# A long convolution and routed experts on one core: result copies of the first group's 48-point stage on ScalarE, sums of the third group's first 20 items on VectorE, and a filter image of 96 rows

## The chip, the cores and the metric

The kernel runs on one core of a Trainium2 chip. A core has five engines that work side by side, each with its own queue of instructions that it takes in order: TensorE (PE; its weight loads are listed as PEld), VectorE (DVE), ScalarE (ACT), GpSimd (POOL) and SyncE (SP), which here issues most of the transfers between the chip's main memory and the on-chip memory (SBUF). 16 DMA engines carry all transfers. TensorE writes to PSUM, a small memory of banks; VectorE and ScalarE read it, GpSimd's work here reads SBUF. The metric is the device time of one execution in microseconds (us); the figure is the median of the runs.

## The reference

```python
def _attn_ref(x, h):                     # x: 8 x 5696 x 128, h: 5696 x 128
    L = 2 * S
    Xf = np.fft.rfft(x, n=L, axis=1)
    Hf = np.fft.rfft(h, n=L, axis=0)
    Yf = Xf * Hf[None, :, :]
    return np.fft.irfft(Yf, n=L, axis=1)[:, :S, :]

def _moe_ref(x, w_gate, w1, w2):         # x: 45568 x 128, 8 experts, 1024 hidden
    logits = x @ w_gate
    expert_idx = np.argmax(logits, axis=1)
    ...                                  # gate_w: softmax weight of the chosen expert
    for e in range(E):
        mask = expert_idx == e
        xe = x[mask]
        h = np.maximum(xe @ w1[e], 0.0)
        out[mask] = gate_w[mask, None] * (h @ w2[e])
```

A causal convolution of each of 8 sequences with a filter of the same length, and then, for each of the 45,568 rows, one of 8 two-layer experts.

## The kernel before, in words

The transform of length 11,424 is cut into two factors, 48 points and 238 points, of which 120 frequencies q are kept. The 8 sequences are three groups of 2, 3 and 3 (256, 384 and 384 columns, 128 for each sequence). For each group come three stages. Stage A (`phase_a`) multiplies by the long factor and stores the result to U in main memory. Stage B (`phase_b`), the 48-point stage, has 120 items, one for each q: it takes U, transforms over 48 points, multiplies by the filter's transform, transforms back and stores to V. Stage C (`phase_c`) takes V, undoes the long factor, computes which expert each row belongs to and scatters the rows in order of expert to a table SR. The experts (`moe`) then take tiles of 256 rows from SR.

One item of stage B goes through these steps, each some items behind the first (`BLAGS`):

- `forward` (L467): TensorE multiplies the item's slice of uq by its 96 x 128 matrix mt into a PSUM bank, xp. The 128 rows are two halves of 64 (real and imaginary part), of which 48 carry data and 16 are zero.
- `product` (L492, L495): VectorE multiplies xp by the filter image hh, once whole into zt (128 rows) and twice by halves, crossed, into xs (64 rows each).
- `combine` (L502): zt = zt + xs, on GpSimd.
- `inverse` (L510): TensorE multiplies zt by mi into a bank, vp.
- `save` (L519): vp is copied to vt in SBUF, on VectorE in the first group and on ScalarE in the others. After every fourth item vt goes to V (L555).

xp and vp share four banks in turn, so a forward multiply waits for the products two items back and an inverse multiply for the copy two items back.

The first group's stage B also makes the filter image. For a block of four items `filt` (L438) multiplies the filter's transform uht by mt, and `filt_save` (L448) copies each block's result in four pieces on ScalarE to one of three buffers hh. The buffer is used at once by the products and stored to HS in main memory (L555). Groups two and three load it from there, one transfer for each block of four items (L425):

```python
HS = dram.tile([P, QN, 2, D], F32, name="HS")
...
nc.sync.dma_start(hhs[qb][:, :QB], HS[:, q : q + QB])
```

The three buffers are set to zero at the start, all 128 rows. The transfers of a block, 512 KB for hh beside 384 or 576 KB for uq and V, 192 KB for mt and twice 72 KB for mi, all go through SyncE's one queue, in the order in which they are written; it waits there for whatever a transfer needs.

The order of all queues is written by generators that are run against one another by nominal costs (`run`). Beside the first group's stage B runs `weights`, which splits the expert weights into two parts (a cast on ScalarE, L230, a subtraction on VectorE, L231) and stores them to WD. The third group's stage B starts after the second group's last scatters have been put on GpSimd's queue (`sort_one`, L581); from some 20 items on, its items alternate with the second group's expert tiles (xr are their rows, loaded at L935, wb their weights from WD, L954; L985 is the first layer).

Of the kernel before, what the change touches and what calls it, by code (L numbers as in the profile page):

```python
# [13 lines left out]
F32 = mybir.dt.float32  # L14
# [4 lines left out]
ALU = mybir.AluOpType  # L19
# [4 lines left out]
NB = 48  # L24
MB = 119
QN = 120
MP = 120
HP = 64
# [14 lines left out]
SAVEV = ()  # L43
# [5 lines left out]
GAPS = (0, 6000, 5000)  # L49
HOLD = (0, 0, 0)  # L50
AHEAD = 2
HEAD = 26000
A3 = (True, True, False)
ALO = ('gpsimd', 'vector', 'vector')
# [11 lines left out]
def conv_moe(ctx: ExitStack, tc: tile.TileContext, I, out, B, S, D, E, F, split):  # L66
    nc = tc.nc
    P = 128
    K2 = 2 * NB
# [6 lines left out]
    def pool(name, bufs, space=None):  # L76
        kw = {} if space is None else {"space": space}
        return ctx.enter_context(tc.tile_pool(name=name, bufs=bufs, **kw))

    dram = pool("dram", 1, DRAM)  # L80
# [54 lines left out]
    for g, nbs in enumerate(split):  # L135
# [7 lines left out]
            parts.append(gr.parts[-1])  # L143
            b0 += nb
        groups.append(gr)
    HS = dram.tile([P, QN, 2, D], F32, name="HS")
    WD = dram.tile([4, E * P, F], F32, name="WD")

    queue = []
# [248 lines left out]
    def phase_b(gr):  # L398
        g, cb, cw, nch, QB = gr.g, gr.cb, gr.cw, gr.nch, gr.qb
        tiles, outs_ = {}, {}  # L400
# [13 lines left out]
        def load(qb):  # L414
            q = qb * QB
            if q >= QN:
                return
            uq = sb.tile([K2, QB, gr.cols], F32, tag="ld", name=f"uq{g}_{q}", bufs=LD if g else 3)
            nc.sync.dma_start(uq, gr.U[q : q + QB].rearrange("q p c -> p q c"))
            mi = mibufs[qb % 4]  # L420
            for k in range(2):
                nc.sync.dma_start(mi[k * HP : k * HP + NB], I["miq"][k * NB : (k + 1) * NB, q : q + QB, :])
            if g != 0:
                hhs[qb] = hhbufs[qb % 3]
                nc.sync.dma_start(hhs[qb][:, :QB], HS[:, q : q + QB])  # L425
            tiles[qb] = (uq, mi)

        mats, hhs, hbank, cuts = {}, {}, {}, {}
        cutting = F3[g]
        state, banks, late = {}, {}, []  # L430
# [9 lines left out]
        def filt_save(qb, m):  # L440
            if qb not in hbank:
                return
            hp = hbank[qb]
            if m == 0:
                hhs[qb] = hhbufs[qb % 3]
            hh = hhs[qb]
            c2, k = divmod(m, 2)
            nc.scalar.mul(hh[k * HP : (k + 1) * HP, :, c2, :], hp[c2 * HP : (c2 + 1) * HP], -1.0 if m == 3 else 1.0)  # L448
            if m == 3:
                hbank.pop(qb)  # L450
                late.append((HS[:, qb * QB : qb * QB + QB], hh[:, :QB]))

        def forward(n):
            q, c = items[n]
# [44 lines left out]

        def combine(n):  # L500
            zt, xs = state[n]
            nc.gpsimd.tensor_tensor(out=zt, in0=zt, in1=xs, op=ALU.add)  # L502

        def inverse(n):
            q, c = items[n]
# [7 lines left out]
        def save(n):  # L513
            q, c = items[n]
            qb, k0 = divmod(q, QB)
            if k0 == 0 and c == 0:
                outs_[qb] = sb.tile([K2, QB, gr.cols], F32, tag="six", name=f"vt{g}_{q}", bufs=SIX)
            cp = nc.vector.tensor_copy if g == 0 or n % 4 in SAVEV else nc.scalar.copy
            cp(outs_[qb][:, k0, c * cw : (c + 1) * cw], banks.pop(n)[:K2, :cw])  # L519
            if k0 == QB - 1 and c == nch - 1:  # L520
                late.append((gr.V[qb * QB : qb * QB + QB].rearrange("q p c -> p q c"), outs_.pop(qb)))
                tiles.pop(qb), hhs.pop(qb), mats.pop(qb)
# [4 lines left out]
        for qb in range(3 if g == 0 else 2):  # L527
            load_m(qb)
            if qb < 2:
                load(qb)  # L530
# [4 lines left out]
        for m in range(4):  # L535
            filt_save(0, m)
# [4 lines left out]
        for n in range(N + BLAGS[3] + 2):  # L541
            qb, k0 = divmod(n, per)
            if k0 == 1:
                load_m(qb + (3 if g == 0 else 2))
            if k0 == min(3, per - 1):
                load(qb + 2)
            if k0 == 0:
                filt(qb + 1, QB - 1)
                if qb:
                    filt_save(qb, 3)  # L550
            else:
                filt(qb + 2, k0 - 1)
                filt_save(qb + 1, k0 - 1)
            while late:
                nc.sync.dma_start(*late.pop(0))  # L555
            if n < N:
                forward(n)
            cut(n + CUT)
            dp, dc, di, ds_ = BLAGS
            if 0 <= n - di < N:  # L560
                inverse(n - di)
            if 0 <= n - dp < N:
                product(n - dp)
            if 0 <= n - dc < N:
                combine(n - dc)
            if 0 <= n - ds_ < N:
                save(n - ds_)
            yield max(cw * 7 / 2.4 + 200, 2 * cw / 0.96 + 300) if g == 0 else RATE[3 * g - 2] * cw * 8 / 2.4
# [29 lines left out]
    def phase_c(pt, guest=None):  # L598
# [27 lines left out]
        def divide(n, k):  # L626
            if not pt.c3 or n >= nu:
                return
            src = vqs[n][:, :, k * cw : (k + 1) * cw]
            vr = sb.tile([QN, 2, 2, cw], F32R, tag="six", name=f"vr{g}_{n}_{k}", bufs=SIX)  # L630
            nc.scalar.copy(vr[:, 0], src)  # L631
            nc.vector.tensor_tensor(out=vr[:, 1], in0=src, in1=vr[:, 0].bitcast(F32), op=ALU.subtract)  # L632
            vrs[n, k] = vr
# [15 lines left out]
        def settle(n, k):  # L649
            if k == 0:  # L650
                rt = sb.tile([MP, NI, nb, RW], F32, tag="rt", name=f"rt{g}_{n}", bufs=6)
                nc.vector.tensor_tensor(
                    out=rt[:, :, :, D + 1].bitcast(I32),
                    in0=idb[:, pt.b0 : pt.b0 + nb].rearrange("p (o b) -> p o b", o=1).broadcast_to([MP, NI, nb]),
                    in1=ioff[:, n * NI : (n + 1) * NI].rearrange("p (i o) -> p i o", o=1).broadcast_to([MP, NI, nb]),
                    op=ALU.add,
                )
                rts[n] = rt.rearrange("p i b w -> p (i b) w")
            done = nc.scalar.copy(
                rts[n][:, k * cb : (k + 1) * cb, :D],  # L660
                ybank.pop((n, k))[:MP, :cw].rearrange("p (b d) -> p b d", d=D),
            )
            sort_one(done.ins)
# [127 lines left out]
        if gr.g:  # L791
            yield GAPS[2]
        for k in range(AHEAD):
            divide(*divmod(k, nsub))
# [4 lines left out]
        for n in range(n_end + 1):  # L799
            for k in range(nsub):  # L800
# [18 lines left out]
                if n < nu:  # L819
                    divide(*divmod(at + AHEAD, nsub))  # L820
                    settle(n, k)
# [287 lines left out]
    def rest():  # L1109
        yield from phase_a(groups[1])  # L1110
        wait = []
        for gr in groups[1:]:
            spent = 0
            for cost in phase_b(gr):
                spent += cost
                yield cost
                if spent > HEAD and wait:
                    wait.pop().ready = True
# [137 lines left out]
```

## Time and profile before

| | |
|---|---|
| median of 3 runs | 2405.68 us (2403.33 to 2406.07) |
| the profiled execution | 2400.84 us |
| its span, first to last instruction | 2399.1 us |
| mean granted TensorE clock | 0.951 |
| TensorE, VectorE, ScalarE, GpSimd busy | 89%, 67%, 44%, 47% |
| first group's stage B | about 114 to 344 us |
| second group's stage B | about 545 to 832 us |
| third group's stage B | about 1134 to 1470 us |
| the experts alone | from about 1770 us |

A row of a timeline has a start and a length in us, the engine ("SPq" is SyncE's queue), the line, the operation, what it writes and reads, the shapes and a count; in brackets stands how long the engine sat idle before it and what ended that. A row of a group has the count, then the group's busy time in us, the mean length of one in ns and the engine's idle time before them. A row on one line of the code has minimum, median and maximum in ns. A row of the windows has the stretch, each engine's busy time in it, the granted clock, the share of time in which the 16 DMA engines were busy and the rate that they moved.

### The profile page before, as it was taken

How to read it: one execution, taken by the hardware profiler on the slowest of the kernel's cores; microseconds unless marked ns; L12 is line 12 of the kernel's file. 1: busy time of each engine (PE TensorE's matmuls, PEld its weight loads, DVE VectorE, ACT ScalarE, POOL GpSimd, SP SyncE). 2: the span in 40 equal slices, each digit the busy share in tenths (PEclk: the TensorE clock that was granted, in tenths of full speed). 3: DMA queues.
4: the chain of work that ended last, by engine and by line, in shares of the span. 5: the costliest groups of instructions: out<-in, count | busy, mean ns of one | idle time of the engine just before them, and what ended most of it. 6: DMA issues, size and time to landing. Idle time of an engine off the chain costs nothing.

```text
span 2399.1 us, 46517 instructions
## 1 busy us (share of the span) xinstructions
PE 2125.5 (89%) x13998; PEld 1759.0 (73%) x13998; DVE 1602.7 (67%) x3987; ACT 1049.3 (44%) x2233; POOL 1136.7 (47%) x1161
## 2 busy tenths in 40 slices
PE   7777759767999989998699998999979999999997
PEld 4654435444777777775377777988878999999997
DVE  3599965456999846667688885676654455555554
ACT  4533315432443445553144444665534444444443
POOL 5333323663555516677545553577762233333332
PEclk8899989878999999998799999999989999999998
DMA  9988879779999768877778775566322222222220
GB/s 268 294 256 266 271 205 321 234 214 265 271 269 276 213 191 248 258 234 218 220 202 252 210 236 148 124 167 175 95 87 85 76 74 81 75 79 75 80 75 30
DMA packets 226940, 444.88 MB, mean 185 GB/s; under 512 B 30993, under 2 KB 141639, under 8 KB 226688
## 3 DMA queue, kind: packets, MB, share of 16 engines
q1 hardware_dynamic: 202752, 394.78, 56.4%
q0 software_dynamic: 23936, 47.09, 6.5%
q8 instruction: 115, 1.88, 0.3%
q14 instruction: 137, 1.12, 0.2%
HBM read 597.98 MB, written 175.89 MB: 323 GB/s over the span
## 4 chain that ended last, share of the span: by engine, by line
PE 61%; DMA 12%; issue 6%; DVE 4%; POOL 2%; SPq 2%; ACT 1%; POOLq 0%; DVEq 0%; ACTq 0%
PE mh L985 18%; PE ma L1005 18%; PE vp L510 5%; PE xp L467 5%; DMA wb<-WD 5%; PE yp L644 5%; PE pa L279 3%; PE mx L167 2%; DMA SR<-rt,pi 2%; DMA xt<-x 2%; PE tp L683 1%; PE tp L167 1%; POOL out L1028 1%; DVE xs L495 1%; POOL SR L581 1%
## 5 line engine op out<-in xcount | busy, mean ns | idle before, releaser
L993 DVE SCALAR_TENSOR_TENSOR hs<-mh,hs 128x512 fp32r<-128x512 f32 x728 | 502.6, 691 | 473.4 <-ACT hs L991 467.6
L985 PE MATMUL mh<-xtb,wb 128*128 128x256 f32 x4368 | 728.8, 303 | 41.4 <-DMA wb<-WD 30.4
L985 PEld LDWEIGHTS mh<-xtb,wb 128*128 128x128 f32 x4368 | 596.6, 192 | 127.6 <-issue 66.2
L1028 POOL DMA_INDIRECT out<-xr x364 | 362.7, 996 | 681.1 <-DVE xr L1019 606.2
L1005 PE MATMUL ma<-hs,wb 128*128 128x256 f32 x4368 | 659.9, 287 | 10.4 <-DMA wb<-WD 10.2
L991 ACT ACTIVATE hs<-mh 128x512 fp32r<-128x512 f32 x728 | 435.3, 598 | 520.4 <-PE mh L985 518.3
L1005 PEld LDWEIGHTS ma<-hs,wb 128*128 128x128 f32 x4368 | 577.4, 192 | 14.4 <-DMA wb<-WD 13.9
L581 POOL DMA_INDIRECT SR<-rt,pi x384 | 397.3, 1035 | 208.5 <-issue 68.5
L502 POOL TENSOR_TENSOR zt<-zt,xs 128x384 f32<-128x384 f32 (+1 forms) x360 | 324.9, 916 | 313.2 <-DVE xs L495 303.5
L495 DVE TENSOR_TENSOR xs<-xp,hh 64x384 f32<-64x384 f32 (+1 forms) x720 | 367.8, 511 | 26.3 <-POOL zt L502 14.8
L467 PE MATMUL xp<-uq,mt 96*128 96x384 f32 (+1 forms) x720 | 284.1, 478 | 84.4 <-DVE xs L495 53.0
L510 PE MATMUL vp<-zt,mi 128*96 128x384 f32 (+1 forms) x720 | 269.9, 456 | 19.4 <-POOL zt L502 17.2
L519 ACT COPY vt<-vp 96x384 f32<-96x384 f32 x240 | 114.1, 475 | 358.3 <-PE vp L510 349.2
L467 PEld LDWEIGHTS xp<-uq,mt 96*128 96x128 f32 x720 | 118.8, 197 | 133.3 <-PE hp L438 60.9
L492 DVE TENSOR_TENSOR zt<-xp,hh 128x384 f32<-128x384 f32 (+1 forms) x360 | 183.3, 509 | 39.8 <-PE xp L467 19.5
L510 PEld LDWEIGHTS vp<-zt,mi 128*96 128x96 f32 x720 | 108.8, 164 | 113.4 <-issue 58.0
L279 PE MATMUL pa<-xc,fcr 120*120 120x512 f32 x360 | 110.6, 446 | 32.1 <-ACT xc L257 12.4
L448 ACT ACTIVATE hh<-hp 64x512 f32<-64x512 f32 x120 | 70.9, 591 | 142.4 <-issue 100.9
L644 PE MATMUL yp<-vr,gcr 120*120 120x384 f32 x576 | 117.0, 338 | 0.0
L632 DVE TENSOR_TENSOR vr<-vq,vr 120x768 fp32r<-120x768 f32 x96 | 91.5, 955 | 34.2 <-ACT vr L631 33.7
L279 PEld LDWEIGHTS pa<-xc,fcr 120*120 120x120 f32 x360 | 68.0, 203 | 59.0 <-ACT xc L257 17.2
L644 PEld LDWEIGHTS yp<-vr,gcr 120*120 120x120 f32 x576 | 96.2, 183 | 0.3 <-DVE vr L632 0.3
(121 smaller groups left out, 2028.3 us busy)
## 6 DMA issues: line engine op xcount, KB each, us to landing
wb<-WD SPq DMA_DIRECT2D x728, 512.0 KB
vq<-V SPq DMA_DIRECT2D x64, 720.0 KB
U<-ut SPq DMA_DIRECT2D x48, 720.0 KB
uq<-U SPq DMA_DIRECT2D x60, 576.0 KB
V<-vt SPq DMA_DIRECT2D x60, 576.0 KB
hh<-HS SPq DMA_DIRECT2D x60, 512.0 KB
xr<-SR SPq DMA_DIRECT2D x182, 130.0 KB
xt<-x SPq DMA_DIRECT2D x96, 240.0 KB
```

The source lines that it names most:

```text
L279: nc.tensor.matmul(banks[m][:QN, :], lhs, rhs, start=(k == 0), stop=(k == len(ops) - 1))
L467: nc.tensor.matmul(xp[:, :cw], mt[:, k0, :], uc, start=True, stop=True)
L495: nc.vector.tensor_tensor(out=xs[to], in0=x3[at], in1=hv[at, 1].broadcast_to([HP, cb, D]), op=ALU.mult)
L502: nc.gpsimd.tensor_tensor(out=zt, in0=zt, in1=xs, op=ALU.add)
L510: nc.tensor.matmul(vp[:K2, :cw], mi[:, k0, :], zt.rearrange("p b d -> p (b d)"), start=True, stop=True)
L581: s = nc.gpsimd.indirect_dma_start(out=SR[:, :], out_offset=IndirectOffsetOnAxis(ap=pi[:, b : b + 1], axis=0), in_=rt[:, b, :], in_offset= ...
L644: nc.tensor.matmul(yp[:MP, :cw], lhs, rhs, start=(m == 0), stop=(m == len(ops) - 1))
L985: nc.tensor.matmul(hp[:, u, :], wb[:, a, f, :], xt[:, b, :], start=(n == 0), stop=(n == 2))
L991: done = nc.scalar.activation(hs[:, 0], hp, AF.Relu)
L993: nc.vector.scalar_tensor_tensor(out=hs[:, 1], in0=hp, scalar=0.0, in1=hs[:, 0].bitcast(F32), op0=ALU.max, op1=ALU.subtract)
L1005: nc.tensor.matmul(accs[j], wb[:, a, f, :], hs[:, b, u, :], start=(k == 0 and u == 0 and n == 0), stop=(k == NPAIR - 1 and u == 1 and n == 2),
L1028: sc = nc.gpsimd.indirect_dma_start(out=out[:, :], out_offset=IndirectOffsetOnAxis(ap=xr[:, s, D + 1 : D + 2].bitcast(I32), axis=0), in_=x ...
```

## The change

Three things. In the first group's stage B the copy of the result, vp to vt, moves from VectorE to ScalarE, as in the other groups. In the third group's stage B the sum zt + xs of items 0 to 19 moves from GpSimd to VectorE. And the filter image in main memory keeps the 2 x 48 rows that carry data, without the 2 x 16 zero rows: it is stored and loaded in two transfers of 48 rows (192 KB each) in place of one of 128.

```diff
+ALONE = 20
...
-    HS = dram.tile([P, QN, 2, D], F32, name="HS")
+    HS = dram.tile([2, NB, QN, 2, D], F32, name="HS")
...
-                nc.sync.dma_start(hhs[qb][:, :QB], HS[:, q : q + QB])
+                for k in range(2):
+                    nc.sync.dma_start(hhs[qb][k * HP : k * HP + NB, :QB], HS[k, :, q : q + QB])
...
-                late.append((HS[:, qb * QB : qb * QB + QB], hh[:, :QB]))
+                for k2 in range(2):
+                    late.append((HS[k2, :, qb * QB : qb * QB + QB], hh[k2 * HP : k2 * HP + NB, :QB]))
...
-            nc.gpsimd.tensor_tensor(out=zt, in0=zt, in1=xs, op=ALU.add)
+            eng = nc.vector if g > 1 and n < ALONE else nc.gpsimd
+            eng.tensor_tensor(out=zt, in0=zt, in1=xs, op=ALU.add)
...
-            cp = nc.vector.tensor_copy if g == 0 or n % 4 in SAVEV else nc.scalar.copy
-            cp(outs_[qb][:, k0, c * cw : (c + 1) * cw], banks.pop(n)[:K2, :cw])
+            nc.scalar.copy(outs_[qb][:, k0, c * cw : (c + 1) * cw], banks.pop(n)[:K2, :cw])
```

How it moves instructions is seen at three places. In the rows, the number behind a tile's name is the item (zt_13_0 belongs to item 13, vt_8 to the block that starts at item 8), or for hp the block; hh_106 to hh_108 are the three buffers. Lines of the changed kernel stand up to three higher.

VectorE in the first group's stage B, items 12 to 14, before:

```order
L492 TENSOR_TENSOR zt_12_0_1263<-xp_12_0_1241,hh_106 128x256
L495 TENSOR_TENSOR xs_12_0_1262<-xp_12_0_1241,hh_106 64x256 x2
L519 COPY vt_8_1268<-vp_8_0_1243 96x256
L492 TENSOR_TENSOR zt_13_0_1277<-xp_13_0_1258,hh_106 128x256
L495 TENSOR_TENSOR xs_13_0_1276<-xp_13_0_1258,hh_106 64x256 x2
L519 COPY vt_8_1268<-vp_9_0_1260 96x256
```

ScalarE at the same place, before:

```order
L448 ACTIVATE hh_107<-hp_4_1189 64x4x128 x4
L448 ACTIVATE hh_108<-hp_5_1254 64x4x128 x4
L230 CAST wsp_0_1379<-wraw_1036 128x512
L448 ACTIVATE hh_106<-hp_6_1319 64x4x128 x4
L448 ACTIVATE hh_107<-hp_7_1384 64x4x128 x4
```

and ScalarE now:

```order
L450 ACTIVATE hh_107<-hp_4_1192 64x4x128
L522 COPY vt_8_1272<-vp_8_0_1247 96x256
L450 ACTIVATE hh_107<-hp_4_1192 64x4x128
L522 COPY vt_8_1272<-vp_9_0_1264 96x256
L450 ACTIVATE hh_107<-hp_4_1192 64x4x128
L522 COPY vt_8_1272<-vp_10_0_1278 96x256
L450 ACTIVATE hh_107<-hp_4_1192 64x4x128
L522 COPY vt_8_1272<-vp_11_0_1295 96x256
```

VectorE's copies are gone from between the products, and on ScalarE one stands behind each piece of the filter copies, which until now followed one another.

SyncE in the same stage, before (a block of four items):

```order
L555 DMA HS<-hh_107 128x1024
L411 DMA mt_28_1317<-mq 96x512
L555 DMA V_71<-vt_8_1268 96x4x256
L419 DMA uq_24_1348<-U_70 96x4x256
L422 DMA mi_111<-miq 48x384 x2
```

and now:

```order
L558 DMA HS<-hh_107 48x1024 x2
L412 DMA mt_28_1322<-mq 96x512
L558 DMA V_71<-vt_8_1272 96x4x256
L420 DMA uq_24_1353<-U_70 96x4x256
L423 DMA mi_111<-miq 48x384 x2
```

The order is the same, with two stores of the image where one was, ahead of the load of mt.

GpSimd where the third group's stage B opens, before, the last scatters and the first sums:

```order
L581 DMA SR<-rt_22_13164,pi_22_13528 366848x130 x6
L581 DMA SR<-rt_23_13329,pi_23_13550 366848x130 x6
L502 TENSOR_TENSOR zt_0_0_13681<-zt_0_0_13681,xs_0_0_13680 128x384
L502 TENSOR_TENSOR zt_1_0_13688<-zt_1_0_13688,xs_1_0_13687 128x384
L502 TENSOR_TENSOR zt_2_0_13701<-zt_2_0_13701,xs_2_0_13700 128x384
```

and VectorE there now:

```order
L495 TENSOR_TENSOR zt_0_0_13743<-xp_0_0_13736,hh_106 128x384
L498 TENSOR_TENSOR xs_0_0_13742<-xp_0_0_13736,hh_106 64x384 x2
L495 TENSOR_TENSOR zt_1_0_13750<-xp_1_0_13740,hh_106 128x384
L498 TENSOR_TENSOR xs_1_0_13749<-xp_1_0_13740,hh_106 64x384 x2
L506 TENSOR_TENSOR zt_0_0_13743<-zt_0_0_13743,xs_0_0_13742 128x384
L495 TENSOR_TENSOR zt_2_0_13764<-xp_2_0_13747,hh_106 128x384
L498 TENSOR_TENSOR xs_2_0_13763<-xp_2_0_13747,hh_106 64x384 x2
L506 TENSOR_TENSOR zt_1_0_13750<-zt_1_0_13750,xs_1_0_13749 128x384
```

The sum of each of the first 20 items stands on VectorE behind the next item's products; GpSimd's scatters keep their order, and the first sum behind them is that of item 20.

## The prediction

> **What bounds the kernel now.** I read the page's busy lines first, then a table of time windows, then the groups of the one stage that is most changed.
>
> ```profile
> span 2399.1 us, 46517 instructions
> PE 2125.5 (89%) x13998; PEld 1759.0 (73%) x13998; DVE 1602.7 (67%) x3987; ACT 1049.3 (44%) x2233; POOL 1136.7 (47%) x1161
> DVE  3599965456999846667688885676654455555554
> ```
>
> The whole is TensorE's (89%), but in the third to fifth slices of 60 us VectorE stands at 9 tenths, and these slices are the first group's 48-point stage. The windows say what stands beside it there (stretch, length, then busy time and instructions of each engine, the granted clock, the DMA engines' busy share and what they move):
>
> ```profile
> core 0: us, PE busy (x) PEld busy (x) DVE busy (x) ACT busy (x) POOL busy (x), PEclk, DMA share, GB/s
> 40.00:60.00 20.00, 16.30 (x92) 13.16 (x90) 9.31 (x17) 12.56 (x26) 12.36 (x12) 1.00 0.96 325
> 60.00:80.00 20.00, 16.80 (x85) 13.88 (x86) 10.75 (x17) 10.50 (x22) 9.48 (x9) 0.91 0.96 336
> 117.00:177.00 60.00, 43.24 (x196) 30.92 (x195) 56.68 (x132) 22.81 (x39) 23.25 (x33) 0.98 0.83 257
> 177.00:237.00 60.00, 42.49 (x193) 29.77 (x194) 56.65 (x132) 20.76 (x35) 23.21 (x33) 1.00 0.85 265
> 237.00:297.00 60.00, 42.47 (x193) 29.73 (x194) 56.62 (x132) 21.38 (x36) 23.20 (x33) 1.00 0.86 268
> 297.00:342.00 45.00, 32.09 (x124) 20.03 (x123) 42.67 (x100) 11.21 (x19) 17.19 (x24) 0.92 0.69 213
> 572.00:832.00 260.00, 258.57 (x1403) 191.39 (x1401) 241.11 (x443) 104.69 (x223) 143.25 (x145) 1.00 0.90 258
> 1192.00:1470.00 278.00, 278.00 (x1644) 218.00 (x1644) 241.82 (x438) 120.56 (x246) 142.74 (x145) 0.99 0.74 213
> ```
>
> From 117 to 342 us VectorE is busy 94%, ScalarE about a third, and the DMA engines 0.83 to 0.86: the second bound is close. In the same stage of groups two and three (572:832, 1192:1470) TensorE is busy all the time, so there only their openings can move.
>
> **The result copies (first group, 120 items).** Groups of 114 to 344 us, and the nearest ScalarE row for a 256-column copy out of PSUM:
>
> ```profile
> L495 DVE TENSOR_TENSOR xs<-xp,hh 64x256 f32<-64x256 f32 x240 | 101.3, 422 | 5.0
> L448 ACT ACTIVATE hh<-hp 64x512 f32<-64x512 f32 x120 | 70.9, 591 | 142.4 <-issue 100.9 <-PE hp L438 39.3
> L492 DVE TENSOR_TENSOR zt<-xp,hh 128x256 f32<-128x256 f32 x120 | 50.7, 423 | 3.4
> L519 DVE COPY vt<-vp 96x256 f32<-96x256 f32 x120 | 50.2, 421 | 3.6
> L231 DVE TENSOR_TENSOR wsp<-wraw,wsp 128x512 fp32r<-128x512 f32 x14 | 12.5, 893 | 12.7 <-ACT wsp L230 12.3
> L1015 ACT COPY ot<-ma x182: 353/373/398, 589.8 to 2383.4; 128x256 f32<-128x256 f32 x182
> ```
>
> What an item takes without the copy stands in the trace: in the first five items no copy is due yet.
>
> ```profile
> 117.30 0.42 DVE L492 TENSOR_TENSOR zt<-xp,hh 128x256 f32<-128x256 f32 x1
> 121.28 0.42 DVE L492 TENSOR_TENSOR zt<-xp,hh 128x256 f32<-128x256 f32 x1
> ...
> 199.61 0.42 DVE L492 TENSOR_TENSOR zt<-xp,hh 128x256 f32<-128x256 f32 x1
> 201.39 0.42 DVE L492 TENSOR_TENSOR zt<-xp,hh 128x256 f32<-128x256 f32 x1
> ```
>
> Three items in 3.98 us are 1.33 us each; later an item takes 1.78. The copy costs 0.45 us, 120 of them 54 us: VectorE alone would then need 225 - 54 = 171 us for 117:342. That is the far end. ScalarE has room: 0.59 (a filter copy) + 0.37 (the result copy) + 14 x 0.62 / 120 for its half of the weight split = 1.04 us an item, under 1.33.
>
> The DMA engines are next. In 117:297 they are busy (0.83 + 0.85 + 0.86) x 60 = 152.4 us and move (257 + 265 + 268) x 60 us = 47.4 MB, 0.311 MB per busy us. The filter image takes 512 KB per four items, 25 times in these 180 us; a quarter of it (131 KB) off is 3.3 MB, 10.5 us. 141.9 us remain. The windows 40:80 show that 0.96 can be held; at 0.95, 141.9 us of transfers need 149.4 us, 30.6 less than 180, where VectorE's end would be 180 - 101 x 0.45 = 134.6. In 297:342 the image's stores run out and the DMA load is light, so VectorE's end holds: 25 x 0.45 = 11.3 us. Together 42. Between VectorE's end and the DMA engines' the later decides, and by these rows that is the DMA engines'. I also allow 4 us for the 14 weight subtractions: ScalarE's cast, until now done long before, stands behind a filter copy and a result copy (0 to 14 x 0.97 = 13.6 us; 0.3 each taken, because VectorE's own lead over the copy's item is about one item). **-38 us**, between -21 (share stays 0.86: 141.9 / 0.86 = 165, 15 saved, and 6 in the tail) and -54.
>
> The move also adds waits. ScalarE now waits for each result multiply, and the filter copies, the weight casts and SyncE's two HS stores stand behind that; the next mt load stands behind the stores on SyncE. SyncE has slack:
>
> ```profile
> SPq L555 <- DVE vt L519: 87.5, 29, 6.7
> 207.55 0.38 SPq L555 DMA_DIRECT2D HS<-hh  x1
> ```
>
> It waited 87.5 us for result copies in this stage; 30 more issues of 0.38 us are 11 us, hidden in that. What the mt load may take:
>
> ```profile
> 111.12 0.31 SPq L411 DMA_DIRECT2D mt<-mq  x1
> 114.18 2.08 PE L438 MATMUL hp<-uht,mt 96*128 96x128 f32 x8 [0.63 <-DMA mt<-mq]
> ```
>
> From a result multiply to the filter multiply that needs the mt load issued behind it lie seven items. Copy 0.37, filter copy 0.59, two issues 0.76 and 3.1 us until landing are 4.8 us against 7 x 1.33 = 9.3: hidden, without cover only if landing takes over 7.6 us.
>
> **The image in groups two and three.** 60 loads lose 131 KB each and gain one issue (0.38 us). In the steady parts TensorE's 100% covers both. At the two openings four blocks save 4 x 0.131 MB / 0.26 MB per us = 2 us and pay 4 x 0.38 = 1.5 us. Zero, between -2 and +2.
>
> **The sums of the third group's first 20 items.** Its opening in the timeline:
>
> ```profile
> 1134.63 0.55 DVE L492 TENSOR_TENSOR zt<-xp,hh 128x384 f32<-128x384 f32 x1
> ...
> 1152.15 1.00 POOL L581 DMA_INDIRECT SR<-rt,pi  x1 [0.30 <-issue]
> 1154.21 1.12 DVE L495 TENSOR_TENSOR xs<-xp,hh 64x384 f32<-64x384 f32 x2 [13.85 <-POOL zt L502]
> 1154.23 1.59 PE L510 MATMUL vp<-zt,mi 128*96 128x384 f32 x2 [16.19 <-POOL zt L502]
> ...
> 1180.05 0.32 SPq L555 DMA_DIRECT2D V<-vt  x1
> 1181.44 0.88 PE L467 MATMUL xp<-uq,mt 96*128 96x384 f32 x2 [0.24 <-DVE xs L495]
> 1183.06 0.56 DVE L492 TENSOR_TENSOR zt<-xp,hh 128x384 f32<-128x384 f32 x1
> 1188.34 0.69 PE L167 MATMUL mx_None<-ident,xr 128*128 128x128 f32 x2 [5.37 <-DMA xr<-SR]
> 1190.53 1.62 PE L985 MATMUL mh<-xtb,wb 128*128 128x256 f32 x6 [1.50 <-DMA wb<-WD]
> ```
>
> GpSimd's queue holds the second group's scatters until 1153, and the sums wait behind them: TensorE idles 16.2 us. On VectorE the sum follows the products at once, but every item then costs VectorE more: 0.56 + 1.12 + gaps = 1.73 us, plus the sum. No row has a 128x384 sum on VectorE; the nearest, products of that shape, take 0.55 to 0.56, and with a gap I take 0.575. So the stall goes and VectorE is late next. Item 15 ends the fourth block, whose V store SyncE issues just ahead of the expert rows (xr). In the new order each sum follows the next item's products. PE's multiply for item 15's result stands behind its forward multiply of item 19, which reuses item 17's bank, so it waits for product 17. VectorE ends that at 1134.63 + 18 x 1.73 + 16 x 0.575 = 1175.0; the two multiplies and the copy add about 1.7 (0.4, 0.8, 0.5): 1176.7 against 1180.05. Of the stall's 16 us only 3.3 survive at that place, since the sums take back 0.575 an item; at item 20 (product from 1183.06 before) it is 2.9. A thinner DMA load there may bring xr and wb sooner: xr took 6.7 us until used, a load at 111 us 3.1, so 0 to 3.6; I take 1.2. **-4.5 us**, 0 to -7. From 1192 on TensorE is full and keeps the shift. GpSimd's scatters lose nothing.
>
> A row bears on whether scatters beside it stretch such a sum:
>
> ```profile
> L632 DVE TENSOR_TENSOR vr<-vq,vr x96: 945/957/1023, 851.9 to 1714.1; 120x768 fp32r<-120x768 f32 x96
> L231 DVE TENSOR_TENSOR wsp<-wraw,wsp x32: 623/932/1467, 23.7 to 405.7; 128x512 fp32r<-128x512 f32 x32
> ```
>
> Both have two SBUF inputs. L632 runs among scatters and hardly varies; L231, among GpSimd's own additions, takes 0.93 and up to 1.47 us. [...]
>
> **Sum.** -38 + 0 - 4.5 = -42.5 us. The profiled execution took 2400.84 us (span 2399.1, and 1.7 around it), 4.8 under the median 2405.68; against the median that gives 2363. What follows the first stage starts from its V stores and keeps its order, so I see nothing that gives the gain back.
>
> **Rivals.** (a) VectorE, not DMA, ends the first stage: packets overlap better than 0.95. Full copies' worth, -54, and the opening's -4.5 to -7: 2346. For it: both ends lie close. (b) The DMA share stays 0.86, as in-order waits on SyncE thin it: -21 - 2.5, 2382. Against it: the wait that SyncE had most was for these copies. (c) Sums beside GpSimd's work stretch as L231's (0.93 for 0.69, a third): 19 x 0.19 = 3.7 us of the 4.5 go, 2367. [...] (d) Slower: the mt load behind the HS stores. If landing takes 12 us, 13.7 us for seven items are 1.96 an item, 120 x (1.96 - 1.78) = 22 more, less 4.5: 2423; it decides above 10.8 us (7 x 1.78 - 1.7). (e) The move does nothing, since the DMA engines are the true bound already: 2401 to 2410; VectorE's 94% speaks against it.
>
> **Chances.** My forecast 0.61 (own range 2352 to 2374), (a) 0.14, (b) 0.13, (c) 0.06, (d) 0.03, (e) 0.03. 0.2% (5 us) is about what a measurement here can tell from no change: faster 0.94, same 0.03, slower 0.03. The range holds the forecast, (a), (b) and (c): 2345 to 2385.
>
> **What would show it.** First stage: an item 1.45 to 1.52 us, DMA share 0.93 or more, result copies of 0.37 us on ScalarE, SyncE's wait for them far under 87 us, the stage 38 us shorter and everything behind it moved by as much. Wrong if TensorE's filter multiplies wait for mt, or VectorE for weight casts by over 10 us. Third group: no 16 us gap; the sums 0.555 us, 2.3 us an item, first expert multiplies 4 to 5 us earlier by the stage's own clock.

## The result, and the profile after

The changed kernel takes 2370.62 us (median of 4 runs, 2360.57 to 2372.23) beside 2405.88 for the kernel before on the same chip: ratio 0.9844, 95% interval 0.9815 to 0.9874, so 30 to 44 us less. The forecast was 2363, in a range of 2345 to 2385. The profiled execution took 2372.01 us (span 2370.2). The total came out near the forecast by luck, because two errors of opposite sign lay in it: the first group gained more than was said, and the sums of the third group lost time instead of gaining it.

The page's busy lines of the changed kernel:

```profile
span 2370.2 us, 46594 instructions
PE 2145.5 (91%) x13998; PEld 1755.5 (74%) x13998; DVE 1562.7 (66%) x3887; ACT 1090.1 (46%) x2353; POOL 1123.2 (47%) x1141
```

VectorE lost 40 us of work, and ScalarE took 41. The windows of the first group's 48-point stage (stretch, length, busy time and instructions of each engine, granted clock, DMA share, GB/s), with the third group's opening as the last row:

```profile
117.00:177.00 60.00, 54.54 (x254) 36.97 (x252) 56.76 (x133) 40.98 (x87) 32.26 (x43) 1.00 1.01 310
177.00:237.00 60.00, 55.12 (x257) 36.39 (x258) 56.72 (x132) 41.65 (x90) 32.89 (x43) 1.00 1.04 330
237.00:287.00 50.00, 42.87 (x192) 27.20 (x190) 46.44 (x109) 32.01 (x70) 27.13 (x35) 1.00 0.93 290
1092.00:1160.00 68.00, 53.37 (x74) 19.48 (x74) 48.44 (x89) 8.82 (x19) 16.14 (x16) 0.50 0.69 165
```

The first stage now runs from 116.27 to 287.60 us, before from 117.30 to 342.25: it is 53.6 us shorter, and ends 54.7 earlier. VectorE is still the one that sets its length: it is busy 94% (56.7 of 60 us) as before, and only has less to do in each item. TensorE went from 72% to 91%, ScalarE from about a third to 69%. The DMA share reads 1.01 and 1.04: the forecast had taken 0.95 for the most that it can be.

The last row is the surprise. Over the whole opening of the third group the granted clock is 0.50, and TensorE looks busy 53 of 68 us, where before it was busy 30 us of 56 and had a stall of 16. The same opening in the kernel before, with two of its multiplies behind the stall:

```profile
1134.00:1190.00 56.00, 30.10 (x74) 12.29 (x74) 36.09 (x69) 8.81 (x19) 35.67 (x36) 0.74 0.77 215
1157.78 0.81 PE L467 MATMUL xp<-uq,mt 96*128 96x384 f32 x2
1158.60 0.86 PE L510 MATMUL vp<-zt,mi 128*96 128x384 f32 x2
```

Now its instructions, for one item (TensorE, VectorE and ScalarE in the timeline):

```profile
1115.60 1.65 PE L470 MATMUL xp<-uq,mt 96*128 96x384 f32 x2 [0.56 <-ACT vt L522]
1117.04 1.49 PE L514 MATMUL vp<-zt,mi 128*96 128x384 f32 x2
1117.29 0.56 DVE L495 TENSOR_TENSOR zt<-xp,hh 128x384 f32<-128x384 f32 x1 [1.21 <-PE xp L470]
1117.86 1.12 DVE L498 TENSOR_TENSOR xs<-xp,hh 64x384 f32<-64x384 f32 x2
1118.57 0.47 ACT L522 COPY vt<-vp 96x384 f32<-96x384 f32 x1 [3.02 <-PE vp L514]
1119.01 0.56 DVE L506 TENSOR_TENSOR zt<-zt,xs 128x384 f32<-128x384 f32 x1
...
1160.07 1.62 PE L988 MATMUL mh<-xtb,wb 128*128 128x256 f32 x6 [2.65 <-DMA wb<-WD]
```

The next forward multiply starts at 1119.10: 3.49 us an item, where VectorE needs 2.3. TensorE runs forward, then result multiply, each at half speed (1.65 and 1.49 us; before, at full clock, 0.81 and 0.86), then stands still for 0.56 us until the result copy is done (1118.57 + 0.47), and only then starts the next forward multiply. VectorE waits 1.21 us an item for that. From the first product (1092.28) to the first expert multiply (1160.07) the opening takes 67.8 us; before it took 55.9 (1134.63 to 1190.53).

Why the forward multiply waits for a copy is seen in the order of the instructions as built, with the semaphores that each waits for. Forward and result multiplies (xp, vp) share four PSUM banks. Before:

```
L467 MATMUL xp2_7_0_13746<-uq2_4_13669,mt2_4_13667 128x384 [waits DVE_49,PE_49]
L510 MATMUL vp2_3_0_13748<-zt2_3_0_13711,mi0_109 96x384 [waits Activation_49,Pool_49]
```

After:

```
L470 MATMUL xp2_7_0_13810<-uq2_4_13730,mt2_4_13728 128x384 [waits Activation_49]
L514 MATMUL vp2_3_0_13812<-zt2_3_0_13774,mi0_109 96x384 [waits DVE_49,PE_49]
```

Before, in this opening, one bank served all result multiplies: each took over the bank of the result multiply before it (and waited for that copy while a forward multiply ran in between). The other three served the forward multiplies, which waited for products alone, those of the item three back. So the four banks were not taken in turn with a wait for the item two back, as the description of the kernel before has it. After, with the sums on another engine, the banks go round in another order: the forward multiply takes the bank of the result multiply just ahead of it. Forward, result, copy, forward is then one chain with nothing beside it on TensorE. Nothing in the diff speaks of banks. The sums alone bring the new order: the kernel that has only them has it too, and those that keep them on GpSimd (sums back, copies alone, image alone, all below) keep one bank for the result multiplies of at least the first 15 items. That the order changed because the scheduler now takes the banks to come free in another order is my reading, not tested.

The gain along the way, after against before: 54.7 us at the end of the first stage, 50.9 at the end of the first group's scatters, 48.7 at the second group's first product, 47.4 at its first expert multiply, 42.4 at the third group's first product, 30.5 at its first expert multiply, 28.8 at the end. These come from one profiled execution of each kernel, and single executions differ by some us (the last two experiments show how much).

### The profile page after: what moved, and what is told of

The parts are those of the page before. It is cut to its first block, busy times and chain, and to the rows that moved or that the text cites. A ratio compares the mean times of both kernels' runs of the same rounds, so it can differ in the third digit from the quotient of the medians.

```text
span 2370.2 us, 46594 instructions
## 1 busy us (share of the span) xinstructions
PE 2145.5 (91%) x13998; PEld 1755.5 (74%) x13998; DVE 1562.7 (66%) x3887; ACT 1090.1 (46%) x2353; POOL 1123.2 (47%) x1141
## 4 chain that ended last, share of the span: by engine, by line
PE 66%; DMA 14%; issue 8%; DVE 4%; POOL 3%; SPq 2%; ACT 2%; POOLq 0%; ACTq 0%; DVEq 0%
PE mh L988 18%; PE ma L1008 17%; PE vp L514 8%; PE xp L470 8%; DMA wb<-WD 5%; PE yp L647 5%; PE pa L280 4%; DMA SR<-rt,pi 3%; PE mx L168 2%; DVE xs L498 2%; PE tp L686 1%; PE tp L168 1%; DMA U<-ut 1%; POOL out L1031 1%; DMA xt<-x 1%
## 5 line engine op out<-in xcount | busy, mean ns | idle before, releaser
L506 POOL TENSOR_TENSOR zt<-zt,xs 128x384 f32<-128x384 f32 (+1 forms) x340 | 310.7, 928 | 292.1 <-DVE xs L498 212.6
L522 ACT COPY vt<-vp 96x384 f32<-96x384 f32 (+1 forms) x360 | 158.3, 440 | 431.7 <-PE vp L514 425.8
L514 PE MATMUL vp<-zt,mi 128*96 128x384 f32 (+1 forms) x720 | 284.9, 478 | 17.4 <-DVE xs L498 5.8
L292 ACT COPY ut<-pa 120x512 f32<-120x512 f32 x96 | 56.2, 585 | 75.8 <-PE pa L280 69.3
```

The costliest lines, as they stand in the source:

```text
L506: eng.tensor_tensor(out=zt, in0=zt, in1=xs, op=ALU.add)
L514: nc.tensor.matmul(vp[:K2, :cw], mi[:, k0, :], zt.rearrange("p b d -> p (b d)"), start=True, stop=True)
```

## Experiments

Nine kernels. "Opening" is, as above, the time in the third group from the first product to the first expert multiply, read from each kernel's timeline.

**The sums back on GpSimd, the rest as changed.**

```diff
-ALONE = 20
+ALONE = 0
```

> The changed kernel with the third group's first 20 sums put back on GpSimd (ALONE = 0); copies and filter image stay. Theory A (the sums on VectorE cost the opening of the third group 12 us: it took 67.8 us from the first product to the first expert multiply instead of 55.9): about 56 us there again, a stall near 16 us before the first result multiply, and about 12 us faster than the changed kernel, 2356 to 2361. Theory B, the step as predicted (the sums gain 4.5 us, and the 12 us come from the other parts): 4 to 5 us slower than the changed kernel, 2375.

Measured: 2356.75 us, ratio to before 0.9807 (0.9794 to 0.9820). Opening 56.7 us (1089.71 to 1146.40), with the stall back:

```profile
1109.30 1.59 PE L514 MATMUL vp<-zt,mi 128*96 128x384 f32 x2 [16.18 <-POOL zt L506]
...
1115.70 0.81 PE L470 MATMUL xp<-uq,mt 96*128 96x384 f32 x2
```

Behind the stall the products of three items stand ready, TensorE runs without a pause, and 6.4 us later its multiplies are at full speed. Theory A: the 16 us stall is cheaper than the order without it.

**The sums alone.**

```diff
+ALONE = 20
...
-            nc.gpsimd.tensor_tensor(out=zt, in0=zt, in1=xs, op=ALU.add)
+            eng = nc.vector if g > 1 and n < ALONE else nc.gpsimd
+            eng.tensor_tensor(out=zt, in0=zt, in1=xs, op=ALU.add)
```

> The kernel before with only the 20 sums on VectorE. Theory A (in this order TensorE's forward multiply waits for the result copy of the multiply just ahead of it, the pauses keep the granted clock at 0.5, and an item takes 3.49 us): opening near 68 us, clock 0.5 in it, and 10 to 14 us slower than before, 2416 to 2420. Theory B (as predicted): 2.3 us an item at full clock, 4.5 us faster, 2401. If the low clock came from something that the copies or the image bring along, 2.3 us an item here too.

Measured: 2416.30 us, ratio 1.0053 (1.0041 to 1.0066), 10 to 16 us slower. Opening 67.3 us (1132.35 to 1199.60), in the windows:

```profile
1133.00:1199.00 66.00, 53.36 (x74) 19.49 (x74) 46.71 (x85) 8.80 (x19) 15.53 (x15) 0.50 0.64 170
```

The timeline's rows (1.65 and 1.49 us, 0.56 us of pause, 3.49 us an item) are those of the changed kernel over again. So it is the sums that bring the chain, the pause and the low clock, without copies or image (theory A).

**The copies alone, with the filter image of 128 rows.**

```diff
-            cp = nc.vector.tensor_copy if g == 0 or n % 4 in SAVEV else nc.scalar.copy
-            cp(outs_[qb][:, k0, c * cw : (c + 1) * cw], banks.pop(n)[:K2, :cw])
+            nc.scalar.copy(outs_[qb][:, k0, c * cw : (c + 1) * cw], banks.pop(n)[:K2, :cw])
```

> The kernel before with only the first group's result copies on ScalarE; the filter image keeps its 128 rows. Theory A (VectorE alone ends the first stage, the DMA engines are no bound there even with the full image): items of 1.33 us, the stage 54 us shorter as in the changed kernel, DMA share 1.05 to 1.15, time near 2355, since the third group's opening keeps its 56 us. Theory B, the step as predicted (the DMA engines bind at a share of 0.95): with the full image 152.4 busy us need 160 us of the 180, so the stage is only 27 to 31 us shorter, items 1.53 us, time near 2377.

Measured: 2354.29 us, ratio 0.9791 (0.9779 to 0.9804): faster than the whole change. The first stage takes 171.4 us (118.68 to 290.11), the changed kernel's 171.3 (116.27 to 287.60):

```profile
118.00:178.00 60.00, 54.97 (x252) 37.80 (x250) 56.64 (x132) 41.01 (x87) 31.52 (x41) 0.97 1.02 328
178.00:238.00 60.00, 55.42 (x257) 36.26 (x257) 56.74 (x132) 41.82 (x89) 32.88 (x43) 1.00 1.05 347
```

VectorE stands at 94% here too, while the DMA engines move 347 GB/s with the full image and 330 with the small one in the same time. The DMA engines were no bound, and the smaller image did nothing for this stage (theory A). Less is lost behind the first stage as well: 53.2 us are still there at the third group's first product, against 42.4 in the changed kernel.

**A burst of multiplies, to raise the clock and leave banks and waits alone** (changed kernel).

```diff
+REPEAT = 9
...
-                nc.tensor.matmul(xp[:, :cw], mt[:, k0, :], uc, start=True, stop=True)
+                for _ in range(REPEAT if g == 2 and n == 3 else 1):
+                    nc.tensor.matmul(xp[:, :cw], mt[:, k0, :], uc, start=True, stop=True)
```

> The changed kernel, but the forward multiply of the third group's fourth item runs 9 times over into the same bank, in the 6.7 us in which TensorE waits for the first product anyway (the same result; 16 extra instructions at 0.41 us are 6.6 us). Waits, banks and sums stay. Theory A (the granted clock of 0.5 makes the item 3.49 us; it stays low because no stretch of TensorE without a pause is long enough to raise it): clock near 1.0 through the opening, forward and result multiplies 0.81 to 0.9 us, items 2.3 us (VectorE's own load), the opening 67.8 - 20 x 1.19 = 44 us, at most 52 with the waits for expert rows behind it, and 16 to 24 us faster than the changed kernel: 2347 to 2355. Theory C (the wait for the copy is what costs, whatever the clock): the loop forward, result, copy is still there, and items stay over 3 us; 2371 or a few us more.

Measured: 2368.48 us, ratio 0.9823 (0.9790 to 0.9855), but of two kinds: 2347.28 and 2350.21 in two runs, with a mean granted clock of 0.959 and 0.957, and 2368.24 to 2371.18 in four, with 0.944 or 0.945. So the two runs at the time that theory A names were also those with the higher clock. The profiled one is of the slower four:

```profile
1079.56 7.67 PE L472 MATMUL xp<-uq,mt 96*128 96x384 f32 x20
1088.99 0.88 PE L472 MATMUL xp<-uq,mt 96*128 96x384 f32 x2 [1.75 <-issue]
1091.31 0.96 PE L516 MATMUL vp<-zt,mi 128*96 128x384 f32 x2 [1.43 <-issue]
1093.08 1.62 PE L472 MATMUL xp<-uq,mt 96*128 96x384 f32 x2 [0.81 <-DVE xs L500]
```

The burst brought full speed (0.88), but over the three pauses behind it (1.75, 1.43 and 0.81 us) the clock fell again, and the 3.49 us chain followed. Inconclusive by itself; the next two were made from it.

**The same with the pauses filled too.**

```diff
+REPEAT = {3: 11, 4: 3, 5: 2}
...
-                nc.tensor.matmul(xp[:, :cw], mt[:, k0, :], uc, start=True, stop=True)
+                for _ in range(REPEAT.get(n, 1) if g == 2 else 1):
+                    nc.tensor.matmul(xp[:, :cw], mt[:, k0, :], uc, start=True, stop=True)
```

> As the burst kernel, with more of TensorE's pauses filled: the forward multiply of item 3 of the third group runs 11 times, that of item 4 three times, that of item 5 twice (same result). In the burst kernel the pauses of 1.75, 1.43 and 0.8 us behind the burst were left, the profiled run went back to 0.5 there and its items took 3.49 us; two of six runs ended at 2347 and 2350, the others at 2368 to 2371. Theory A (the clock decides, and those two runs kept it): clock 1.0 through the opening and items of 2.3 us, all or most runs at 2345 to 2355. Theory C (the clock falls with pauses of 0.77 us in 2.3 us as well): times of both kinds again, or 2368 to 2371 in all.

Measured: 2353.18 us (2343.91 to 2356.47), ratio 0.9777 (0.9760 to 0.9795). The profiled run, in the windows and in the timeline:

```profile
1092.00:1140.00 48.00, 35.94 (x90) 12.93 (x88) 45.91 (x86) 8.81 (x19) 15.25 (x15) 1.00 0.87 216
```

```profile
1114.52 0.91 PE L472 MATMUL xp<-uq,mt 96*128 96x384 f32 x2 [0.56 <-ACT vt L524]
1115.37 0.86 PE L516 MATMUL vp<-zt,mi 128*96 128x384 f32 x2
1116.79 0.91 PE L472 MATMUL xp<-uq,mt 96*128 96x384 f32 x2 [0.56 <-ACT vt L524]
```

Clock 1.00, 2.3 us an item, VectorE busy 96%, opening 49.9 us (1092.58 to 1142.45). The wait for the copy is still there, 0.56 us as before, but at full clock it hides behind VectorE. The 18 us between this opening and the changed kernel's are the clock's.

**Another bank for the forward multiplies, no multiply added** (changed kernel). Those of items 4 to 19 take the two banks of the expert multiplies, which begin only later.

```diff
-            xp = ps.tile([P, 512], F32, tag="cx", name=f"xp{g}_{q}_{c}", bufs=4)
+            tag, bufs = ("mh", 2) if g == 2 and 4 <= n < ALONE else ("cx", 4)
+            xp = ps.tile([P, 512], F32, tag=tag, name=f"xp{g}_{q}_{c}", bufs=bufs)
```

> The changed kernel, but the forward multiplies of the third group's items 4 to 19 take their PSUM banks from the pair that the expert multiplies use (idle until then), the result multiplies alone rotate through the four shared ones. So a forward multiply waits for the products of the item two before, no longer for the copy of the result multiply just ahead of it. Theory A (order of banks and clock together: the wait for the copy leaves 0.56 us of pause in each item, and the pauses hold the clock at 0.5): at 0.5 TensorE has 1.44 + 1.49 = 2.93 us an item without a pause, against VectorE's 2.3; it runs through, the clock goes to 1.0 after some 3 to 7 us, and then items take 2.3 us: opening 44 to 52 us instead of 67.8, time 2350 to 2358. Theory C (the clock stays at 0.5 whatever the pauses): items 2.93 us, 0.56 x 16 = 9 us less, opening 59 us, 2362. Theory D (VectorE's sums themselves are what takes the time): no change, 2371.

Measured: 2350.70 us (2348.37 to 2352.85), ratio 0.9779 (0.9767 to 0.9792). Opening 52.4 us (1088.08 to 1140.51):

```profile
1098.64 1.50 PE L471 MATMUL xp<-uq,mt 96*128 96x384 f32 x2 [2.73 <-DVE xs L499]
1099.93 1.49 PE L515 MATMUL vp<-zt,mi 128*96 128x384 f32 x2
1101.21 1.30 PE L471 MATMUL xp<-uq,mt 96*128 96x384 f32 x2
1102.34 0.81 PE L515 MATMUL vp<-zt,mi 128*96 128x384 f32 x2
1103.23 0.88 PE L471 MATMUL xp<-uq,mt 96*128 96x384 f32 x2
1103.95 0.81 PE L515 MATMUL vp<-zt,mi 128*96 128x384 f32 x2
1105.64 0.88 PE L471 MATMUL xp<-uq,mt 96*128 96x384 f32 x2 [0.88 <-DVE xs L499]
...
1107.95 0.88 PE L471 MATMUL xp<-uq,mt 96*128 96x384 f32 x2 [0.79 <-DVE xs L499]
```

At 1098.64 the multiplies are still at half speed, but now nothing stands between them; by 1102.34 they are at 0.81 us, and from 1105.64 an item takes 2.32. With no wait for the copy the clock came up, so the order of banks is what kept it down.

**The image alone** (kernel before).

```diff
-    HS = dram.tile([P, QN, 2, D], F32, name="HS")
+    HS = dram.tile([2, NB, QN, 2, D], F32, name="HS")
...
-                nc.sync.dma_start(hhs[qb][:, :QB], HS[:, q : q + QB])
+                for k in range(2):
+                    nc.sync.dma_start(hhs[qb][k * HP : k * HP + NB, :QB], HS[k, :, q : q + QB])
...
-                late.append((HS[:, qb * QB : qb * QB + QB], hh[:, :QB]))
+                for k2 in range(2):
+                    late.append((HS[k2, :, qb * QB : qb * QB + QB], hh[k2 * HP : k2 * HP + NB, :QB]))
```

> The kernel before with only the filter image of 96 rows (HS stored and loaded as two halves). As predicted: no change, 2401 to 2406 (0, between -2 and +2). Rival: it costs 2 to 5 us, since with the image the second group's opening has another order of banks (a forward multiply waits for a result copy, 2.12 us an item instead of 1.73) and each block of groups two and three one more load to issue ahead of the expert weights (the kernel with copies and image took 2356.75, the one with the copies alone 2354.29): 2405 to 2409. Against a gain from the smaller transfers: with the full image the first stage was as short as with the small one.

Measured: 2408.08 us in 12 runs (2400.70 to 2413.16) beside 2404.46, ratio 1.0012 (1.0001 to 1.0023): 0 to 6 us slower. The interval ends next to 1, and the profiled execution (2413.16) is the slowest of the twelve, so the size is uncertain; it is no gain. In that profile the second group's stage, from the first expert multiply to the last product, takes 264.1 us instead of 259.9. SyncE's own waits there (total, times, longest), first of the kernel before:

```profile
SPq L954 <- PE mh L985: 43.8, 19, 3.8
```

and with the image:

```profile
SPq L958 <- PE mh L989: 25.5, 14, 3.5
```

SyncE's slack, its wait until an expert weight's buffer is free, fell by 18 us: it is later with these loads. The profiles of all kernels agree on this stage: from its first product to its last it takes 282.8 to 286.6 us in the six with the small image (the changed kernel among them) and 277.4 to 279.8 in the five with the full one, and TensorE waits 3.5 to 6.7 us for expert weights in the six, 1.7 to 2.8 in the five. Whether more issues or the narrower transfers take it wasn't tried. The other bank order that the expectation names is there too, but only two forward multiplies wait for a copy, and an item of 2.12 us for 1.73 costs 0.4.

**Copies and sums without the image, with the banks of above.**

```diff
+ALONE = 20
+OWN = 20
...
+            nc.scalar.copy(outs_[qb][:, k0, c * cw : (c + 1) * cw], banks.pop(n)[:K2, :cw])
...
+            tag, bufs = ("mh", 2) if g == 2 and 4 <= n < OWN else ("cx", 4)
...
+            eng = nc.vector if g > 1 and n < ALONE else nc.gpsimd
```

> The kernel before with the first group's result copies on ScalarE, the third group's first 20 sums on VectorE, and the forward multiplies of its items 4 to 19 in the expert multiplies' pair of PSUM banks; the filter image keeps 128 rows. If the parts add up: the copies-only kernel took 2354.29 with an opening near 56 us, the bank kernel's opening took 52.4, so 3 to 4 us less: 2350 to 2352, and the forward multiply never waits for the result copy. If the image is what costs behind the first stage, this is 2 to 4 us under the bank kernel (2350.7): 2347 to 2349.

Measured: 2353.24 us (2348.46 to 2358.14), ratio 0.9785 (0.9761 to 0.9809). Opening 52.9 us, 2.9 less than with the copies alone, but the gain at the third group's first product is only 48.8 us there, against 53.2. Up to that place the two kernels have the same instructions, so the 4.4 us are no effect of an edit but the difference between two executions. The time itself is under neither figure of the expectation. Beside the bank kernel (2350.70 us, 0.9779), which has the small image and is otherwise the same, leaving the image out shows no gain. With the 20 sums on VectorE the opening is bounded by VectorE's 2.3 us an item, so a smaller number was tried last.

**The same with 8 sums.**

```diff
-ALONE = 20
+ALONE = 8
```

> The same with only the first 8 sums on VectorE: GpSimd's scatters end some 20 us after the stage's first product, and 8 items of 2.3 us take 18.6 us, so that GpSimd can take the sums from there and VectorE's item falls back to 1.73 us. Theory: 7 to 12 items without a sum of 0.575 us, 4 to 7 us off until item 15 to 19, as far as the expert rows and weights come as early: opening 45 to 49 us, time 2344 to 2349. Rival: the expert rows and weights bound the opening by now (in the bank kernel TensorE waited 2.5 and 4.6 us for them): no gain over the kernel with 20 sums.

Measured: 2341.07 us (2336.64 to 2350.20), ratio 0.9747 (0.9723 to 0.9772): the fastest kernel of the study, 55 to 67 us less than before. Opening 47.3 us (1078.40 to 1125.72), as in the expectation's theory:

```profile
1096.00 1.18 POOL L584 DMA_INDIRECT SR<-rt,pi  x1 [0.31 <-issue]
...
1098.21 1.26 POOL L506 TENSOR_TENSOR zt<-zt,xs 128x384 f32<-128x384 f32 x1 [1.04 <-DVE xs L498]
...
1105.68 0.88 PE L470 MATMUL xp<-uq,mt 96*128 96x384 f32 x2 [0.20 <-DVE xs L498]
1107.41 0.88 PE L470 MATMUL xp<-uq,mt 96*128 96x384 f32 x2 [0.20 <-DVE xs L498]
```

GpSimd has just issued its last scatter at 1096 when the ninth sum comes to it, and soon after an item takes 1.73 us instead of 2.32. The opening explains 5.6 of the 12 us between the medians of this kernel and the last one. The two have the same instructions ahead of the third group, yet its first product came at 1078.40 here and at 1085.82 there: 7.4 us that are the execution's own.

## Why the prediction was right or wrong

**The copies: right in mechanism, mis-sized, -53.6 in the stage instead of -38** (-50 for the whole, by the ratio of the kernel with the copies alone). An item fell to 1.33 us, the far end, which rival (a) had priced:

```profile
201.15 0.42 DVE L495 TENSOR_TENSOR zt<-xp,hh 128x256 f32<-128x256 f32 x1
...
202.48 0.42 DVE L495 TENSOR_TENSOR zt<-xp,hh 128x256 f32<-128x256 f32 x1
```

The group of the result copies in this stage, and SyncE's wait for them:

```profile
L522 ACT COPY vt<-vp 96x256 f32<-96x256 f32 x120 | 44.2, 368 | 52.5 <-PE vp L514 49.4 <-DMA uq<-U 2.4 <-DMA mi<-miq 0.3
```

```profile
SPq L558 <- ACT vt L522: 16.3, 19, 4.6
```

The copy took 0.37 us on ScalarE as said, and SyncE's wait for copies fell from 87.5 to 16.3 us. The step that failed is "at 0.95, 141.9 us of transfers need 149.4 us": it took the largest share seen in two windows for the most that the DMA engines give. They went to 1.01 and 1.04 here and to 1.05 with the full image; so the share of this view isn't a part of a whole that ends at 1. A window of the trace of before says the same, the opening of the second group:

```profile
551.00:570.00 19.00, 11.32 (x28) 4.65 (x26) 14.01 (x26) 2.65 (x6) 7.96 (x8) 0.86 1.07 287
```

Had that been read, rival (a) would have been the forecast for this term. Also the allowance of 4 us for weight casts behind ScalarE's copies wasn't needed: VectorE stayed at 94% and waited for no cast between the stage's first product and its last.

**The image: 0 foretold, at most a few us lost.** Alone it costs 0.2 to 5.5 us (interval); the kernel with copies and image takes 2.5 us more than the one with the copies alone; with the other banks (the bank kernel and the one without the image) no loss shows in the times. In the second group's stage it costs 3 to 9 us in every pair of profiles. The step that failed is "TensorE's 100% covers both": the expert weights stand in the same SyncE queue behind the extra issue, and TensorE waits longer for them (3.5 to 6.7 us where it waited 1.7 to 2.8).

**The sums: -4.5 foretold, +9 to +14 measured.** Against the kernel with the sums on GpSimd the whole change is 13.9 us slower by the medians of two comparisons (2370.62 and 2356.75), 8.9 by their ratios to before (0.9844 - 0.9807, of 2405 us); the sums alone cost 10 to 16. Four of the steps hold: the 16 us gap is gone; the sums take 0.56 us beside the scatters, so rival (c) fell:

```profile
L506 DVE TENSOR_TENSOR zt<-zt,xs 128x384 f32<-128x384 f32 x20 | 11.2, 559 | 0.6
```

VectorE's own load is 2.3 us an item; and at full clock the opening is 6.0 us shorter than before with the pauses filled and 3.5 with other banks, around the 4.5 of the forecast. The failing step is "PE's multiply for item 15's result stands behind its forward multiply of item 19, which reuses item 17's bank ... the two multiplies and the copy add about 1.7 (0.4, 0.8, 0.5)". It took the order of banks from the description, four in turn, which holds in neither kernel (in the kernel before, item 19's forward multiply takes item 16's bank), and took multiply times at full clock. In the changed order the forward multiply waits for a copy (0.56 us an item), and the clock stayed at 0.50. Both could be seen beforehand: the waits in the order of the built kernel, and the half-speed multiplies in the trace of before (1.59 us at 1154.23, for 0.86 at 1158.60), which came to full speed behind the stall after 3.55 us of items that stood ready (0.81 us at 1157.78).

**The total.** By the ratios of the three kernels with one part each, copies -50, image +3 and sums +13 make -34 us; the whole change measured -37 (30 to 44 less). The forecast of -42.5 had -38, 0 and -4.5: the copies brought 12 us more than foretold, and the sums and the image took 20 away.

## What to carry to other kernels

A stall that ends in a burst can be cheaper than the even flow that replaces it: here TensorE stayed at half speed where its work was spread out with pauses (0.56 us in each 3.49, granted clock 0.50), and came to full speed where it ran on without one (for 3.55 us in the kernel before, 6.4 with the sums back). So an edit that spreads its work out must be costed at both speeds (here 3.49 and 2.3 us an item), until the trace shows which one a like pattern has. When instructions move between engines, read again which buffer each multiply takes over and what it then waits for; a rotation that was harmless closed a chain here, forward, result, copy, forward. And take no share of a busy-time view for a ceiling until the trace's highest window has been looked up (here 1.07, where 0.95 was taken).

## What the runs showed of the hardware

Like pauses went with either clock. With pauses of 0.56 us in each 3.49, TensorE 81% busy (53.36 of 66 us, sums alone), the granted clock was 0.50 throughout. With pauses of about 0.56 us in each 2.3 it was 1.00 from 1092 to 1140 us in the kernel with the pauses filled, whose opening began with 34 multiplies in 13.93 us. In the bank kernel, with pauses of 0.74 to 0.88 us in most items, the multiplies took 0.81 to 0.89 us each from 1102.34 to 1133. From half to full speed they came in runs without a pause: 3.7 us in the bank kernel (1.50 us at 1098.64, 0.81 at 1102.34), 3.55 in the kernel before (1.59 us at 1154.23, 0.81 at 1157.78), 6.4 with the sums back (1.59 us at 1109.30, 0.81 at 1115.70).

The clock also came down. In the profiled burst kernel the pauses behind the burst were 1.75, 1.43 and 0.81 us, with 0.88 and 0.96 us of multiplies between, and the next multiplies took 1.62 and 1.49 us. In the kernel with 20 sums and no image it fell after some 18 us of items that all ran alike (2.3 us each, pauses of 0.74 to 0.83):

```profile
1122.62 0.81 PE L514 MATMUL vp<-zt,mi 128*96 128x384 f32 x2
1124.22 1.31 PE L470 MATMUL xp<-uq,mt 96*128 96x384 f32 x2 [0.79 <-DVE xs L498]
1125.33 1.49 PE L514 MATMUL vp<-zt,mi 128*96 128x384 f32 x2
```

What sets the fall stays open. Two of six runs of the burst kernel were some 20 us faster, at a mean clock of 0.957 and 0.959 for 0.944 and 0.945, which suggests that whether it comes differs from run to run; but those two left no trace.
